# Interleaving transposes with low-part attention products, and splitting four more half heads, in a fused attention and MoE kernel on one Trainium2 core

## Chip, cores and metric

One core of a Trainium2 chip runs the whole kernel. The metric is the device time of one execution in microseconds (us); less is better.

## What is computed

The reference runs causal attention with a distance bias, then two feed-forward blocks, on 4 batches x 8 heads x 576 positions x 64 dimensions:

```python
scores = scale * np.matmul(q, k.transpose(0, 1, 3, 2))
cum = np.cumsum(np.maximum(s, 0.0), axis=-1)
bias = -(cum[:, :, :, None] - cum[:, :, None, :])
scores = np.where(causal, -1000000000.0, scores + np.minimum(bias, 0.0))
scores = scores - np.max(scores, axis=-1, keepdims=True)
attn = np.exp(scores)
attn = attn / (np.sum(attn, axis=-1, keepdims=True) + 1e-09)
x = np.matmul(attn, v)          # -> 2304 tokens x 512
h = ((x @ w1) * (x @ w2)) @ w3  # 1024 wide
x = h @ w_out                   # 512
h = x @ w_in                    # 2048
out = (h - np.tanh(h)) @ w_out2
```

## The kernel before

**Numbers.** Nearly all products run as fp32r matmuls on values split in two parts: a high part (a rounded copy) and a low part (value minus high part), made by a copy on ACT or DVE and a subtraction on DVE or POOL (`split`). The first batch's attention is the exception: there the heads run in full fp32 (`full`), which needs no split, and each fp32 product is shown as two matmuls in the trace.

**Attention.** A head has five tiles of queries (`QT`: 64, 128, 128, 128, 128 rows), in two groups: group 0 is tiles 0 to 2 (queries 0 to 319), group 1 is tiles 3 and 4. Per tile: the scores go to one of two PSUM banks (L589 when full, L591 and L592 when split); DVE adds the mask and takes the row minimum (L602); ACT takes the exponential (L608) into the buffer `e`; `flip` transposes `e` in chunks of 128 columns on TensorE (L638) into one of three banks, up to four to a bank, and copies them out to `en` (full) or splits them to `eh` and `el`. Per group, `pv` then multiplies by the values: full, L673 on `en`; split, first the high part on `eh` with 128 stationary columns (the two parts of V side by side, L675), then the low part on `el` with 64 stationary columns (L678), three matmuls for group 0 (320, 256 and 128 columns wide) and five for group 1 (four of 256, one of 128). L685 adds the two halves of the bank.

**Order of heads.** Batch 0 runs group 0 of its eight heads, then group 1 of its eight heads, all full. Then come the heads of batch 1 (again group 0 of all, then group 1 of all) and of batches 2 and 3 (both groups together), all split. Split heads use two sets of buffers in turn; the set of the odd heads lies in a pool that opens only when batch 0's heads are done. The products of a batch with w1 and w2 (`products`, L737, three matmuls of 288 columns to an operation) follow its attention at a lower priority, beside the next batch's attention. The weights w1 and w2 are decoded from doubles in 16 chunks (L431 to L437: one ACT and four DVE instructions each, then a split) at priorities around those of the first heads: the number `convp` sets where. After the attention come w3 folded into w_out, the product with that, and the second feed-forward block, which fills the span from about 590 us on.

**Who sets the order.** A planner (`Plan.order`) schedules the whole program with a cost for each operation, taking on each engine the ready operation of the lowest priority number; `emit` then writes the instructions in order of planned start. A `pv` or a bank of transposes is one operation. Where the planner finds TensorE idle in the first 150 us it puts in filler matmuls (L506), which compute nothing. Engines run in the order written.

Of the kernel before, what the change touches and what calls it, by code (L numbers as in the profile page):

```python
# [16 lines left out]
P = 128  # L17
B, H, S, D = 4, 8, 576, 64
# [16 lines left out]
XT = [(t, min(t + 512, NT)) for t in range(0, NT, 512)]  # L35
MASKED8 = -8.0e9
NR = D + 10
PARAM = dict(ramp0=50.0, ramp1=50.0, byf=(0,), dsub=1000.0, dsub0=1000.0, dcopy=1000.0, dcopy0=600.0, dother=1000.0, dother0=1000.0, spi=500.0, lay=6, lay0=4, layp=2.2e5, layf=2.95e5, gate=0, dve0=1000.0, early=100.0e3, raw0=0, rawp=-700.0, ng=3, nosb=2, cut=(1,), convq=1200.0, natb=8, abk=1, wap=0.95e6, dve=1000.0, act=0.0, pool=0.0, sem=160.0, pesem=180.0, slow=1.1, convp=590.0, npre=4,
             nbias=3, keep=0.5, ff=0.0, fu=150.0e3, wlast=8, bw=370.0, ntr=3, actb=1, actn=0, spp=-80.0, ne=2, nsb=2, ncf=5, outlag=15)

LO_CLAMP = 2.0 ** -15 * 1.125
# [19 lines left out]


class Op:
    __slots__ = ("opts", "eng", "lat", "fn", "prio", "deps", "succ", "n", "ready", "start", "end", "dur", "as_", "ae", "two", "kind", "bank")


class Plan:
# [11 lines left out]
        self.BIAS = {"DVE": PARAM["dve"], "ACT": PARAM["act"], "POOL": PARAM["pool"]}  # L79
        self.ops = []  # L80

    def op(self, opts, r=(), w=(), prio=0.0, lat=0.0, two=False, kind=None):
        o = Op()
        o.kind = kind
        o.two = two
        o.opts = {e: (d, fn) for e, d, fn in opts}
        o.prio, o.lat, o.eng = prio, lat, None
        o.bank = None
        for x, items in (("r", r), ("w", w)):
            if any((it[0] if isinstance(it, tuple) else it) is self.fill_bank for it in items):  # L90
                o.bank = x
        o.deps = set()
        for which, items in ((0, r), (1, w)):
            for it in items:
                b, parts = it if isinstance(it, tuple) else (it, range(it.n))
                for i in ([parts] if isinstance(parts, int) else parts):
# [12 lines left out]
        self.ops.append(o)  # L109
        return o  # L110
# [20 lines left out]
    def order(self):  # L131
# [34 lines left out]
        while True:  # L166
# [35 lines left out]
            if e == "PE":  # L202
                while self.fill_from < free[e] and free[e] + 110.0 < t < self.fill_until and not unread and free[e] >= read:
                    f = Op()
                    f.eng, f.fn, f.start, f.prio, f.lat, f.deps = e, self.filler, free[e], 9e9, 0.0, ()
                    f.dur = 107.0 * self.clock(free[e])
                    f.end = f.start + f.dur
                    self.busy(f.start, f.end)
                    done.append(f)
                    free[e] = f.end  # L210
                t = max(t, free[e])
# [22 lines left out]
        return sorted(range(len(done)), key=lambda i: (done[i].start, i))  # L234

    def emit(self):
        for i in self.order():
            self.done[i].fn()


def c_pe(n, m=P):
# [24 lines left out]
def tile_kernel(ctx, tc, qk, v, s, w1, w2, w3t, w_out, w_in, w_out2, out):  # L266
    nc = tc.nc
# [76 lines left out]
    def dve(fn, n, r, w, prio, fast=False, two=False, extra=0.0):  # L344
        pl.op([("DVE", c_dve(n, fast) + extra, fn)], r=r, w=w, prio=prio, two=two or fast)

    def pe(cost, fn, r, w, prio):
        pl.op([("PE", cost, fn)], r=r, w=w, prio=prio)


    nat = Pool("nat", "right")
# [187 lines left out]
    def head(h, full, groups=(0, 1)):  # L539
# [87 lines left out]
        def flip(t):  # L627
            q0, q1 = QT[t]
            nq = q1 - q0
            nch = (q1 + P - 1) // P  # L630
            p_ = pr + 10 * t + 50
            for js in [list(range(min(4, nch)))] + ([[4]] if nch > 4 else []):
                bk = tr_ring.next()
                rows = D if js == [4] else P

                def tr(bk=bk, js=js, rows=rows):
                    for n, c in enumerate(js):
                        nc.tensor.transpose(bk.t[:rows, n * P:(n + 1) * P], e.t[:, EOFF[t] + c * P:EOFF[t] + c * P + rows], ident.t)  # L638
                pe(109.0 * len(js), tr, [(e, t), ident], [bk], p_)
                n = len(js)  # L640
                if js == [4]:
                    view = lambda d: d.t[:D, eb + 1024:eb + 1024 + P]
                    src = lambda bk=bk: bk.t[:D, 0:P]
                else:
                    o = q0 if t < 3 else eb + q0 - 320
                    if n == 1:
                        view = lambda d: d.t[:, o:o + nq]
                        src = lambda bk=bk: bk.t[:, 0:nq]
                    else:
                        view = lambda d, n=n: d.t[:, o:o + 256 * n].rearrange("p (c q) -> p c q", q=256)[:, :, 0:nq]  # L650
                        src = lambda bk=bk, n=n: bk.t[:, 0:n * nq].rearrange("p (c q) -> p c q", q=nq)
                if full:
                    copy(lambda view=view: view(en), src, n * nq, [bk], [(en, t)], p_, psum=True)
                else:
                    split(lambda view=view: view(eh), (eh, t), lambda view=view: view(el), (el, t), src, n * nq, [bk], p_, psum=True)

        def pv(grp):
# [9 lines left out]
            X = xf[(h // 2) % 2]  # L667
            o = (h % 2) * D

            def mm():  # L670
# [5 lines left out]
                if not full:  # L676
                    for j, (c, a, w_, kk) in enumerate(lst):
                        nc.tensor.matmul(bk.t[:D, n - w_:n], V.t[:kk, c, 0:D], el.t[:kk, a:a + w_], start=False, stop=j == last, skip_group_check=True)  # L678
            if full:
                pe(sum(c_pe4(w_) for _, _, w_, _ in lst), mm, [RV, (en, parts)], [bk], p_)  # L680
                copy(lambda: X.t[o:o + D, q0:q0 + n], lambda: bk.t[:D, :n], n, [bk], [(X, h % 2)], p_, psum=True)
            else:
                pe(sum(c_pe(w_) + c_pe(w_, D) for _, _, w_, _ in lst), mm, [V, (eh, parts), (el, parts)], [bk], p_)
                copy(lambda: pvt.t[:, :n], lambda: bk.t[D:, :n], n, [bk], [pvt], p_, psum=True)
                dve(lambda: nc.vector.tensor_tensor(X.t[o:o + D, q0:q0 + n], bk.t[:D, :n], pvt.t[:, :n], op=ALU.add), n, [bk, pvt], [(X, h % 2)], p_)  # L685

# [62 lines left out]
                    [cs], [(c_d, b * 2 + half)], 0)  # L749

    for h in range(H):
        head(h, True, (0,))
    for half in range(2):
        for k in range(KC):
            for src, hb, lb in ((w1, w1h, w1l), (w2, w2h, w2l)):
# [5 lines left out]
    for h in range(H + 1):  # L761
        if h == PARAM["natb"]:
            nat.close()
            pl.op([("X", 0.0, lambda: None)], w=[eh])
            spl.open()
            constants(1)
        if h < H:
            head(h, h < PARAM["natb"], (1,))
    for b in range(B):
        if b + 1 < B:  # L770
            for g in ((0,), (1,)) if b + 1 in PARAM["cut"] else ((0, 1),):
# [182 lines left out]
```

## Time and profile before

| | |
|---|---|
| median of 3 runs | 980.98 us (977.44 to 984.19) |
| profiled execution | 975.06 us, span of its instructions 973.3 us |
| TensorE busy (matmul) | 958.5 us, 98% of the span, 5619 matmuls |
| DVE, ACT, POOL busy | 699.6 (72%), 597.6 (61%), 384.2 us (39%) |
| granted TensorE clock | 0.999 over the span |

"Busy" of TensorE counts a matmul from its first column to its last result; matmuls overlap, so what one costs is read from the distance between starts, not from its duration. The profiled execution is one run, 0.6% under the median of the three.

### The profile page before, as it was taken

Reading aid. Unit: us, or ns where it says so; the run is one execution under the profiler, and the core shown is the slowest. Engines: PE = TensorE matmul, PEld = TensorE weight load, DVE = VectorE, ACT = ScalarE, POOL = GpSimd, SP = SyncE. Lnnn points to the kernel's source line nnn. Section 1 sums busy time; section 2 is a strip of 40 time slices with the busy share of each in tenths; the row PEclk is TensorE's granted clock in tenths of the full one; section 3 lists DMA queues with packets and bytes.
Section 4 is the critical chain, followed back from the end, with each engine's and each line's share of the span. In section 5 each row is a group of like instructions: output and inputs, shape, how many; then the busy total and the mean of one; then the engine's idle time right before and its main releaser. Section 6 shows DMA issues by size and latency. Waiting matters only on the chain.

```text
span 973.3 us, 16442 instructions
## 1 busy us (share of the span) xinstructions
PE 958.5 (98%) x5619; PEld 832.9 (86%) x5619; DVE 699.6 (72%) x1421; ACT 597.6 (61%) x1360; POOL 384.2 (39%) x330
## 2 busy tenths in 40 slices
PE   8999999999999999999999999999999999999998
PEld 6667899999999999889888898878888888888897
DVE  7888868889889759996596897984454555454554
ACT  5777677888888744443444457555556555645565
POOL 3444566535535333422454548432222222222222
PEclk9999999999999999999999999999999999999999
DMA  6665455654545135568488782212003000200010
GB/s 184 187 189 173 132 169 180 200 193 124 174 143 158 45 105 178 176 204 285 136 312 286 249 274 81 65 55 77 1 0 110 21 1 1 87 0 1 1 44 23
DMA packets 69162, 122.22 MB, mean 126 GB/s; under 512 B 6651, under 2 KB 38656, under 8 KB 69078
## 3 DMA queue, kind: packets, MB, share of 16 engines
q1 hardware_dynamic: 69078, 121.17, 39.0%
q8 instruction: 44, 0.72, 0.3%
q14 instruction: 40, 0.33, 0.1%
HBM read 91.43 MB, written 25.99 MB: 121 GB/s over the span
## 4 chain that ended last, share of the span: by engine, by line
PE 89%; DVE 4%; DMA 3%; issue 2%; ACT 1%; POOL 1%; SPq 0%; DVEq 0%; ACTq 0%; POOLq 0%
PE bank L879 19%; PE bank L737 18%; PE bank L902 6%; PE bank L900 6%; PE bank L901 6%; PE bank L638 5%; PE bank L842 3%; PE bank L841 3%; PE bank L843 3%; PE bank L673 3%; PE bank L589 2%; PE bank L675 2%; PE bank L678 2%; PE bank L592 2%; PE bank L591 2%
## 5 line engine op out<-in xcount | busy, mean ns | idle before, releaser
L334 POOL TENSOR_TENSOR gl<-pg,gh 128x512 fp32r<-128x512 f32 (+1 forms) x78 | 98.8, 1266 | 260.8 <-ACT gh L328 234.3
L879 PE MATMUL bank<-x2b,wih 128*128 128x512 f32 (+1 forms) x640 | 182.4, 370 | 0.0
L890 DVE TENSOR_TENSOR pg<-bank,u 128x512 f32<-128x512 f32 (+1 forms) x80 | 50.8, 635 | 142.1 <-ACT th L889 138.0
L879 PEld LDWEIGHTS bank<-x2b,wih 128*128 128x128 f32 x640 | 116.7, 188 | 21.7
L879 PE MATMUL bank<-x2b,wil 128*128 128x512 f32 (+1 forms) x320 | 117.9, 368 | 0.0
L902 PE MATMUL bank<-voh,gl 128*128 128x512 f32 x288 | 113.1, 393 | 0.4 <-POOL gl L334 0.4
L900 PE MATMUL bank<-voh,gh 128*128 128x512 f32 x288 | 113.0, 392 | 0.2 <-ACT gh L328 0.2
L901 PE MATMUL bank<-vol,gh 128*128 128x512 f32 x288 | 112.6, 391 | 0.0
L328 ACT ACTIVATE gh<-pg 128x512 fp32r<-128x512 f32 (+1 forms) x80 | 47.1, 589 | 87.0 <-DVE pg L894 85.9
L608 ACT ACTIVATE e<-e,nmx 64x64 f32<-64x64 f32 (+4 forms) x160 | 88.6, 555 | 7.6 <-DVE nmx L602 6.9
L887 ACT ACTIVATE u<-bank 128x512 f32<-128x512 f32 (+1 forms) x80 | 44.4, 555 | 71.6 <-PE bank L879 65.4
L737 PE MATMUL bank<-xh,w2h 128*128 128x288 f32 x256 | 81.4, 318 | 1.3 <-DVE cst L745 1.3
L737 PE MATMUL bank<-xh,w1h 128*128 128x288 f32 x256 | 81.3, 318 | 0.7 <-ACT asb L328 0.5
L602 DVE CUSTOM_DVE_ANT_0 e<-bank,msk 64x64 f32<-64x64 f32 (+4 forms) x160 | 64.4, 418 | 21.1 <-PE bank L592 14.0
L431 ACT ACTIVATE wt<-wraw 128x512 f32<-128x512 f32 x72 | 47.9, 670 | 50.5 <-DMA wraw<-w_out 14.1
L638 PE MATMUL bank<-ident,e 128*128 128x128 f32 (+1 forms) x480 | 78.5, 274 | 0.2
L737 PE MATMUL bank<-xh,w2l 128*128 128x288 f32 x256 | 75.5, 295 | 0.0
L737 PE MATMUL bank<-xh,w1l 128*128 128x288 f32 x256 | 75.5, 295 | 0.0
L737 PE MATMUL bank<-xl,w1h 128*128 128x288 f32 x256 | 75.5, 295 | 0.0
L737 PE MATMUL bank<-xl,w2h 128*128 128x288 f32 x256 | 75.4, 295 | 0.0
L894 DVE COPY_PREDICATED pg<-mk,th 128x512 f32<-128x512 uint32 (+1 forms) x80 | 62.6, 783 | 13.6 <-ACT mk L892 5.7
L879 PEld LDWEIGHTS bank<-x2b,wil 128*128 128x128 f32 x320 | 60.3, 188 | 10.5
(139 smaller groups left out, 2589.2 us busy)
## 6 DMA issues: line engine op xcount, KB each, us to landing
rqk<-qk SPq DMA_DIRECT2D x24, 576.0 KB
wraw<-w_out SPq DMA_DIRECT2D x24, 512.0 KB
c_d<-cst SPq DMA_DIRECT2D x32, 288.0 KB
wraw<-w SPq DMA_DIRECT2D x16, 512.0 KB
wraw<-w3t SPq DMA_DIRECT2D x16, 512.0 KB
cf<-c_d SPq DMA_DIRECT2D x32, 256.0 KB
wraw<-w_in SPq DMA_DIRECT2D x16, 512.0 KB
x_d<-x2s SPq DMA_DIRECT2D x16, 512.0 KB
```

Of the source, the lines that this page charges most:

```text
L334: o.append(("POOL", c_pool2(n), lambda: nc.gpsimd.tensor_tensor(dst(), a(), b().bitcast(F32), op=ALU.subtract)))
L431: act(lambda: nc.scalar.activation(tf(), h32().bitcast(F32), AF.Abs), 512, [r_], [t_], prio)
L602: nc.vector.tensor_tensor_reduce(e.t[:nq, EOFF[t] + k0:EOFF[t] + k1], bk.t[:nq, :k1 - k0], bi.t[:nq, bo + k0:bo + k1], -0.125, 3.0e38 if f ...
L608: act(lambda: nc.scalar.activation(et(), et(), AF.Exp, bias=nmx.t[:nq, i, tm:tm + 1], scale=-1.0, accum_out=ssum.t[:nq, pj, t, i:i + 1]), ...
L638: nc.tensor.transpose(bk.t[:rows, n * P:(n + 1) * P], e.t[:, EOFF[t] + c * P:EOFF[t] + c * P + rows], ident.t)
L737: nc.tensor.matmul(bk.t[:, :HALF], w_.t[:, k, f * P:(f + 1) * P], x_.t[:, k, o:o + HALF], start=k == 0 and j == 0, stop=k == KC - 1 and j ...
L879: nc.tensor.matmul(bk.t[:, :w], w_.t[:, k, a], X2.t[:, i, k, :w], start=k == 0 and n == 0, stop=k == KC - 1 and n == 2)
L890: dve(lambda u=u, pg=pg, hp=hp, c_=c_: nc.vector.tensor_tensor(c_(pg), hp(), c_(u), op=ALU.mult), w, [bk, u], [pg], pr)
L894: dve(lambda pg=pg, mk=mk, th=th, c_=c_: nc.vector.copy_predicated(c_(pg), c_(mk).bitcast(U32), c_(th)), w, [mk, th], [pg], pr, two=True)
L900: nc.tensor.matmul(bank[n].t, gh.t[:, a], voh[f].t, start=f == 0, stop=False)
L901: nc.tensor.matmul(bank[n].t, gh.t[:, a], vol[f].t, start=False, stop=False)
L902: nc.tensor.matmul(bank[n].t, gl.t[:, a], voh[f].t, start=False, stop=f == NF2 - 1)
```

## The change

Three things change. First, `flip` and `pv` hand the planner their parts: each transpose by itself, and a split `pv` as its high part and a list of low matmuls. `emit` then looks, for each split `pv`, at the next 8 operations on TensorE in the planned order (`ahead=8`). A bank of transposes among them is moved up if by the plan its data (and its bank) are there by the end of that `pv` (`zipw=1.0`), until there are as many transposes as low matmuls. The high part is written first, and then low matmuls and transposes in turn; the planned times stay as they are. Second, four half heads of batch 0 are split instead of full: group 0 of head 6 (`part0=(6,)`) and group 1 of heads 2, 4 and 6 (`part1=(2, 4, 6)`). Third, `convp` goes from 590 to 690, which puts the decoding of w1 and w2 later by one head's priority.

```diff
     def emit(self):
-        for i in self.order():
-            self.done[i].fn()
+        seq = [self.done[i] for i in self.order()]
+        pe = [o for o in seq if o.eng == "PE" and o.fn is not self.filler]
+        at = {o: max([d.end + d.lat + (0.0 if d.eng == "PE" else self.SEM["PE"]) for d in o.deps], default=0.0) for o in pe if o.kind == "tr"}
+        idx = {o: n for n, o in enumerate(seq)}
+        used, zipped = set(), {}
+        for i, a in enumerate(pe):
+            if a.kind != "pv":
+                continue
+            turns = []
+            for b in pe[i + 1:i + 1 + PARAM["ahead"]]:
+                if len(turns) >= len(a.parts[1]) or any(d in pe[i + 1:i + 1 + PARAM["ahead"]] and d not in used for d in b.deps):
+                    break
+                if b.kind == "tr" and b not in used and a not in b.deps and at[b] <= a.start + PARAM["zipw"] * a.dur and all(idx[d] < idx[a] for d in b.deps):
+                    turns += b.parts
+                    used.add(b)
+            zipped[a] = turns
...
+        for o in seq:
+            if o in zipped:
+                first, last = o.parts
+                first()
+                for n in range(max(len(last), len(zipped[o]))):
+                    for x in (last, zipped[o]):
+                        if n < len(x):
+                            x[n]()
+            elif o not in used:
+                o.fn()
...
     for h in range(H):
-        head(h, True, (0,))
+        head(h, h not in PARAM["part0"], (0,))
...
-            head(h, h < PARAM["natb"], (1,))
+            head(h, h < PARAM["natb"] and h not in PARAM["part1"], (1,))
```

## Rows read from the trace of the kernel before

**Rows 1.** The page's list of engines: busy us, share, instructions.

```profile
PE 958.5 (98%) x5619; PEld 832.9 (86%) x5619; DVE 699.6 (72%) x1421; ACT 597.6 (61%) x1360; POOL 384.2 (39%) x330
```

**Rows 2.** Stretches: length, then busy us (instructions) of each engine; clock, DMA.

```profile
25.00:50.00 25.00, 23.62 (x158) 16.25 (x157) 20.27 (x58) 19.23 (x62) 10.70 (x11) 1.00 0.63 184
50.00:75.00 25.00, 24.44 (x147) 17.39 (x146) 22.01 (x49) 19.52 (x45) 10.78 (x12) 1.00 0.69 196
75.00:100.00 25.00, 25.00 (x148) 18.77 (x148) 21.80 (x55) 18.49 (x48) 12.44 (x12) 1.00 0.53 157
100.00:125.00 25.00, 24.45 (x191) 22.83 (x190) 20.12 (x56) 15.53 (x53) 14.17 (x17) 1.00 0.47 131
...
425.00:450.00 25.00, 24.44 (x164) 22.90 (x163) 18.69 (x32) 9.61 (x18) 8.54 (x6) 1.00 0.88 286
```

**Rows 3.** Stretches of 50 to 100 us, fillers (L506) alone, summed.

```profile
sum 50.00, PE 2.34 PEld 1.90; mean PE 0.47 PEld 0.38
```

**Rows 4.** Matmuls in order of time, 68 to 74 us: start, us, name.

```profile
68.69 2.16 PE L673 MATMUL bank<-en,rv 128*64 128x256 f32 x10
70.78 0.66 PE L638 MATMUL bank<-ident,e 128*128 128x128 f32 x4
71.27 0.92 PE L589 MATMUL bank<-rqk 69*128 69x448 f32 x2
72.03 0.27 PE L617 MATMUL bank<-ident,ssum 128*4 128x128 f32 x1
...
72.58 0.65 PE L589 MATMUL bank<-rqk 69*128 69x288 f32 x2
73.06 0.27 PE L638 MATMUL bank<-ident,e 128*64 128x128 f32 x1
```

**Rows 5.** Matmuls in order of time, 255 to 262 us: the same pieces, split.

```profile
255.45 0.30 PE L591 MATMUL bank<-kh,qs 128*128 128x288 f32 x1
...
255.72 0.30 PE L737 MATMUL bank<-xh,w2h 128*128 128x288 f32 x1
...
256.79 0.69 PE L675 MATMUL bank<-eh,vs 128*128 128x256 f32 x5
257.31 0.69 PE L678 MATMUL bank<-el,vs 128*64 128x256 f32 x5
257.85 0.49 PE L638 MATMUL bank<-ident,e 128*128 128x128 f32 x3
...
261.00 0.37 PE L591 MATMUL bank<-kh,qs 128*128 128x448 f32 x1
...
261.41 0.27 PE L638 MATMUL bank<-ident,e 128*64 128x128 f32 x1
```

**Rows 6.** DVE groups of 150 to 340 us: count, busy us, mean ns, idle before.

```profile
L332 DVE TENSOR_TENSOR el<-bank,eh 128x512 fp32r<-128x512 f32 x45 | 29.5, 680 | 0.5 <-ACT eh L328 0.3
...
L685 DVE TENSOR_TENSOR xf<-bank,pvt 64x256 f32<-64x256 f32 x23 | 9.5, 412 | 6.5 <-ACT pvt L328 6.2
...
L332 DVE TENSOR_TENSOR el<-bank,eh 64x128 fp32r<-64x128 f32 x23 | 6.4, 277 | 0.1
```

**Rows 7.** Waits of TensorE in 0 to 160 us: total, times, longest.

```profile
PE bank L589 <- DMA rqk<-qk: 1.0, 2, 0.6
```

**Rows 8.** Weight loads in order of time, 258 us, behind three transposes.

```profile
258.06 0.14 PEld L591 LDWEIGHTS bank<-kh,qs 128*64 128x64 f32 x1
258.17 0.14 PEld L592 LDWEIGHTS bank<-kl,q 74*64 74x64 f32 x1
258.23 0.19 PEld L591 LDWEIGHTS bank<-kh,qs 128*128 128x128 f32 x1
258.34 0.19 PEld L592 LDWEIGHTS bank<-kl,q 74*128 74x128 f32 x1
```

**Rows 9.** Matmuls at 254 us: three low matmuls, then one transpose.

```profile
254.00 0.48 PE L678 MATMUL bank<-el,vs 128*64 128x320 f32 x3
254.32 0.28 PE L638 MATMUL bank<-ident,e 128*128 128x128 f32 x1
```

**Rows 10.** Weight load that starts when the product behind that transpose does.

```profile
254.44 0.19 PEld L737 LDWEIGHTS bank<-xl,w2h 128*128 128x128 f32 x1
```

**Rows 11.** All transposes of attention: what TensorE sat idle for before them.

```profile
  ACT e L608: 0.3, 2
```

More of the change, by code (lines that the diff above doesn't have):

```diff
@@ L37 @@
 NR = D + 10
-PARAM = dict(ramp0=50.0, ramp1=50.0, byf=(0,), dsub=1000.0, dsub0=1000.0, dcopy=1000.0, dcopy0=600.0, dother=1000.0, dother0=1000.0, spi=500.0, lay=6, lay0=4, layp=2.2e5, layf=2.95e5, gate=0, dve0=1000.0, early=100.0e3, raw0=0, rawp=-700.0, ng=3, nosb=2, cut=(1,), convq=1200.0, natb=8, abk=1, wap=0.95e6, dve=1000.0, act=0.0, pool=0.0, sem=160.0, pesem=180.0, slow=1.1, convp=590.0, npre=4,
+PARAM = dict(ahead=8, zipw=1.0, part0=(6,), part1=(2, 4, 6), ramp0=50.0, ramp1=50.0, byf=(0,), dsub=1000.0, dsub0=1000.0, dcopy=1000.0, dcopy0=600.0, dother=1000.0, dother0=1000.0, spi=500.0, lay=6, lay0=4, layp=2.2e5, layf=2.95e5, gate=0, dve0=1000.0, early=100.0e3, raw0=0, rawp=-700.0, ng=3, nosb=2, cut=(1,), convq=1200.0, natb=8, abk=1, wap=0.95e6, dve=1000.0, act=0.0, pool=0.0, sem=160.0, pesem=180.0, slow=1.1, convp=690.0, npre=4,
              nbias=3, keep=0.5, ff=0.0, fu=150.0e3, wlast=8, bw=370.0, ntr=3, actb=1, actn=0, spp=-80.0, ne=2, nsb=2, ncf=5, outlag=15)
@@ L63 @@
 class Op:
-    __slots__ = ("opts", "eng", "lat", "fn", "prio", "deps", "succ", "n", "ready", "start", "end", "dur", "as_", "ae", "two", "kind", "bank")
+    __slots__ = ("opts", "eng", "lat", "fn", "prio", "deps", "succ", "n", "ready", "start", "end", "dur", "as_", "ae", "two", "kind", "bank", "parts")
 class Plan:
@@ L80, in __init__, with op @@
         self.ops = []
-    def op(self, opts, r=(), w=(), prio=0.0, lat=0.0, two=False, kind=None):
+    def op(self, opts, r=(), w=(), prio=0.0, lat=0.0, two=False, kind=None, parts=None):
         o = Op()
+        o.parts = parts
         o.kind = kind
@@ L204, in order @@
                     f = Op()
+                    f.kind = f.parts = None
                     f.eng, f.fn, f.start, f.prio, f.lat, f.deps = e, self.filler, free[e], 9e9, 0.0, ()
@@ L236, in emit @@
     def emit(self):
-        for i in self.order():
-            self.done[i].fn()
+        seq = [self.done[i] for i in self.order()]
[14 more added lines that the diff above has]
+            zipped[a] = turns
+        self.nzip = (len(used), sum(min(len(a.parts[1]), len(t)) for a, t in zipped.items()), len(zipped))
+        for o in seq:
[8 more added lines that the diff above has]
+                o.fn()
 def c_pe(n, m=P):
@@ L345, in dve, with pe @@
         pl.op([("DVE", c_dve(n, fast) + extra, fn)], r=r, w=w, prio=prio, two=two or fast)
-    def pe(cost, fn, r, w, prio):
-        pl.op([("PE", cost, fn)], r=r, w=w, prio=prio)
+    def pe(cost, fn, r, w, prio, kind=None, parts=None):
+        pl.op([("PE", cost, fn)], r=r, w=w, prio=prio, kind=kind, parts=parts)
     nat = Pool("nat", "right")
@@ L634, in flip, with tr @@
                 rows = D if js == [4] else P
[L636 to L639, printed above, removed]
+                def tr(bk=bk, rows=rows, n=0, c=0):
+                    nc.tensor.transpose(bk.t[:rows, n * P:(n + 1) * P], e.t[:, EOFF[t] + c * P:EOFF[t] + c * P + rows], ident.t)
+                trs = [lambda tr=tr, n=n, c=c: tr(n=n, c=c) for n, c in enumerate(js)]
+                pe(109.0 * len(js), lambda trs=trs: [f() for f in trs], [(e, t), ident], [bk], p_, kind="tr", parts=trs)
                 n = len(js)
@@ L668, in pv, with low @@
             o = (h % 2) * D
+            def low(j, c, a, w_, kk):
+                nc.tensor.matmul(bk.t[:D, n - w_:n], V.t[:kk, c, 0:D], el.t[:kk, a:a + w_], start=False, stop=j == last, skip_group_check=True)
+            lows = [lambda j=j, x=x: low(j, *x) for j, x in enumerate(lst)]
             def mm():
@@ L675, in mm @@
                         nc.tensor.matmul(bk.t[:, n - w_:n], V.t[:kk, c, :], eh.t[:kk, a:a + w_], start=j == 0, stop=False, skip_group_check=True)
-                if not full:
-                    for j, (c, a, w_, kk) in enumerate(lst):
-                        nc.tensor.matmul(bk.t[:D, n - w_:n], V.t[:kk, c, 0:D], el.t[:kk, a:a + w_], start=False, stop=j == last, skip_group_check=True)
             if full:
@@ L682, in pv @@
             else:
-                pe(sum(c_pe(w_) + c_pe(w_, D) for _, _, w_, _ in lst), mm, [V, (eh, parts), (el, parts)], [bk], p_)
+                pe(sum(c_pe(w_) + c_pe(w_, D) for _, _, w_, _ in lst), lambda: [f() for f in [mm] + lows], [V, (eh, parts), (el, parts)], [bk], p_, kind="pv", parts=(mm, lows))
                 copy(lambda: pvt.t[:, :n], lambda: bk.t[D:, :n], n, [bk], [pvt], p_, psum=True)
```

## The prediction

> **What bounds the kernel now.** I read the list of engines first: the matmul engine is busy for 98% of the span, the next one, DVE, for 72% [rows 1]. Then I cut the span into stretches, because a share over 973 us hides stages. TensorE is full in all of them but the first 50 us [rows 2]; what it can lose is work or filler, not waiting. The attention of the later batches never lets it idle, since the products with w1 and w2 stand behind every head at a lower priority and fill the gaps. So a microsecond of matmul work removed anywhere after some 50 us shortens the kernel by about that, as long as there is other work ready in its place. The end of the stage in which the products finish, 425 to 450 us, bears this out: DVE is at 18.69 of 25 us there and TensorE at 24.44 [rows 2], so the stage ends on matmuls. Between 50 and 100 us, where three of the four half heads stand, TensorE is full too, with 2.34 us of fillers in it [rows 3]; but DVE is at 22.01 and 21.80 of 25 us [rows 2], its heaviest stretch of that part of the kernel.
>
> **The half heads of group 1 (heads 2, 4 and 6).** Full, one costs TensorE from start to start: the ten value matmuls 70.78 - 68.69 = 2.09 us, the scores of 448 columns 72.03 - 71.27 = 0.76, and twice the scores of 288 columns, 73.06 - 72.58 = 0.48 each [rows 4]. That is 2.09 + 0.76 + 0.96 = 3.81 us. Split, the same pieces cost 257.31 - 256.79 = 0.52 (high) and 257.85 - 257.31 = 0.54 (low), 261.41 - 261.00 = 0.41 for 448 columns and twice 255.72 - 255.45 = 0.27 [rows 5]: 2.01 us. The transposes are the same. The saving is 1.80 us each, 5.4 us in all, on the engine that is full.
>
> Against it stands DVE. A split half head adds two subtractions out of PSUM of 0.68 us and one of 0.28 (only DVE does these), and the addition of the two halves, 0.41 [rows 6]: 2.05 us, 6.2 us for three. Copies of q, k and v, and their subtractions, go to ACT and POOL for the most part, which have 12 and 27 us idle in 50 to 100 us [rows 2]. DVE has 3.0 + 3.2 = 6.2 us idle there [rows 2]. It would fill them exactly if the stretch stayed as long as it is, and the stretch is to become 5.4 us shorter. So some DVE work must move behind 100 us, where 4.9 of the next 25 us are idle [rows 2]; the decoding of weights can move, since it feeds products and not the heads, and `convp` moves it. What can't move is the order within a head: the row minimum waits behind a subtraction on DVE, the exponential behind that, the transposes behind both. Ends: nothing of the 5.4 us is lost, or all of it (TensorE then runs fillers or waits, for DVE). Products ready to fill are few here, because those of the second half of the rows need all heads of this group. I take 2.0 us as lost, near the shorter end, because the decoding can be put off.
>
> The DMA queue of SP: a split half head of group 1 loads 576 KB of q and k instead of 288, and it has one load each of `kl` and `q2` where the full one has two of `rel`, so the count is the same. The load of `q2` waits for a copy, and behind it in SP's order stand the next heads' loads and the weights. DMA is at 0.69 and 0.53 of its time [rows 2], and 0.9 MB more at 180 GB/s are 5 us of 50; I price it at nothing, with up to 1 us if a head waits as two did at the start [rows 7].
>
> **Head 6 of group 0.** It has 576 columns of scores where a group 1 has 448 + 288 + 288 = 1024, and 704 of values where that has 1152, so by estimate it saves TensorE 0.6 of the 1.80 us, 1.1 us. It stands at 37 to 50 us, where matmuls wait for the heads' own chain (25 to 50 us is TensorE's emptiest full stretch, 23.62 with fillers counted as busy [rows 2]). A shorter matmul there becomes a filler, and DVE gets some 0.6 x 2.05 = 1.2 us more. I price it at nothing, between -1.1 and +1.2 us. Moving the decoding later by one head costs nothing while products are not short, up to 1.5 us if the few products that run before 60 us come later.
>
> **The turns.** The question is what a transpose costs, and where. The three transposes at 257.85 us are 0.11 us apart: the third starts with its successor's load at 258.06 [rows 5, 8]. Is that its stream or its load? A load runs while the matmul ahead of it streams, and the next load starts when its own matmul takes over the array. Behind the third transpose stands a matmul with 64 stationary columns, whose load starts at 258.06; it takes over at 258.17, when the next load starts [rows 8]. It is 64 wide and holds the array for 0.06 us, its successor's load being 64 wide; the one after it holds 0.11, with a load of 128 columns behind it [rows 8]. So a load of 64 columns needs at most 0.06 us, and yet the transpose ahead of such a load held 0.11: that is its own stream. From the other side, a single transpose between three low matmuls and a product starts at 254.32 and the product takes over at 254.44 [rows 9, 10]; the low matmuls keep their 0.32 us, although the last streams only 128 columns and would not have hidden a load of 0.11.
>
> The low matmul of 256 columns costs (0.54 - 0.06) / 4 = 0.12 us, its stream, its load of 64 columns hidden. In turns, then: low 0.12 with the transpose's load behind it, transpose 0.11 with a low load behind it. In groups it is the same 0.12 + 0.11. **The turns save nothing on TensorE.** What is left is an end effect: the last low matmul (0.06 us) hides a transpose's load but not one of 128 columns (0.11), so 0.05 us hangs on what follows each of 48 low groups. Most are followed by a transpose before; after, those with fewer transposes than low matmuls are not. At most 0.05 x 48 = 2.4 us either way, and since gains and losses mix I take 0.
>
> The turns add a risk. A transpose is written as soon as the first low matmul, when its data need only be there by the planned end of the `pv`, some 0.4 us later. If it is late, TensorE stands, and everything behind it, since it runs in order. Before, transposes waited for the exponential twice, 0.3 us in all [rows 11], so data are mostly early. Ends: 0 and 52 x 0.4 = 21 us; I take 0.5 us, next to the row.
>
> **Sum.** -5.4 + 2.0 + 0 + 0 + 0.5 = -2.9 us on the profiled execution's 975.06 us, 972.2 us. The median of the runs lies 5.9 us above that execution, so I predict 980.98 - 2.9 = 978.1 us. The runs spread over 6.7 us; 1% (9.8 us) is about what a measurement of this kernel can tell from no change.
>
> **Rivals.** (a) *The load is what a transpose waits for.* Then in turns its load hides under a low matmul's stream and a transpose costs about 0.055 us, saving 0.055 per pair. There are at most 4 pairs in a group 1 and 2 in a group 0: 24 x 6 + 14 = 158, 8.7 us; with partners for two in three, 5.8 us, giving 980.98 - 2.9 - 5.8 = 972.3 us. For it speaks that 0.11 us is also exactly what a load of 128 columns takes [rows 8]; against it, the transpose that held 0.11 ahead of a 64-column load. The Trainium skill, TensorE: Matmul & The Clock Gate, section LDWEIGHTS, says that a load lasts as long as its columns at 1.2 GHz, whatever the rows; by that a transpose's 128 columns would be the 107 ns between transposes, and this rival would hold. The trace agrees for the scores and not for the transposes. Chance 0.15.
>
> (b) *DVE takes the place of TensorE between 50 and 110 us.* The saved matmul time turns into fillers and waits for the row minimum or for `el`; DVE's 6.2 us of new work against 6.2 us of idle time decide. The time would be 981 us, or up to 2 us more with head 6's part. Chance 0.25.
>
> (c) *Transposes stand in front of their data.* The place is TensorE's order in each `pv`; the price is up to 0.4 us for each of 52. From 0.06 us each it eats the gain of 2.9 us, at 0.3 us each the kernel needs 980.98 - 3.4 + 15.6 = 993 us, slower than before. For it speaks that the planner's times are estimates and that the window admits data that come at the end of the `pv`; against it, the two short waits before. Chance 0.08.
>
> (d) *Few turns happen* (most transposes near a `pv` belong to tiles not ready): then (a) and (c) shrink and the sum stays, which is why it has no price of its own.
>
> **How the numbers follow.** My forecast has a chance of 0.5, rival (b) 0.25, (a) 0.15, (c) 0.08, the rest something else. The forecast's own range, with the terms' ends and the spread of runs, is 973 to 983. With (a) below and (b) above, and the near part of (c), 967 to 986 holds eight in ten. Faster by over 1% (under 971.2) needs (a) with nearly all pairs, or all terms at their good ends: 0.17. Slower by over 1% (over 990.8) needs (c): 0.08. Within 1%: 0.75.
>
> **What the profile after would show.** Right: 36 matmuls of L673 fewer (ten for each group 1, six for head 6), no idle time before L638 to speak of, low matmul and transpose together still 0.22 to 0.23 us in turns, products starting earlier than before from 60 us on, DVE above 22 of 25 us between 50 and 100 us with the decoding ending some microseconds later. A pair of 0.17 us in turns would prove (a). More than 5 us of fillers and waits in 50 to 110 us would prove (b); idle time before L638 named after the exponential would prove (c). The prediction goes wrong most easily in the size of what DVE gives back.

## The result, and the profile after

The changed kernel takes 984.72 us (median of 7 runs, 981.74 to 991.98) against 978.14 us of the kernel before beside it (7 runs, 973.66 to 984.19): ratio 1.0067, 95% interval 1.0043 to 1.009. It is 6.6 us slower, where 2.9 us less was forecast. The profiled execution takes 984.89 us, span 983.2.

The list of engines [rows 1], and the stretches of 25 us [rows 2], of after:

```profile
PE 961.5 (98%) x5645; PEld 837.9 (85%) x5645; DVE 709.1 (72%) x1437; ACT 601.5 (61%) x1370; POOL 397.2 (40%) x344
```
```profile
25.00:50.00 25.00, 21.41 (x151) 14.93 (x149) 21.31 (x61) 17.55 (x56) 10.77 (x13) 1.00 0.65 190
50.00:75.00 25.00, 23.52 (x153) 17.50 (x152) 22.65 (x54) 19.49 (x48) 13.97 (x15) 1.00 0.65 193
75.00:100.00 25.00, 24.31 (x160) 20.34 (x159) 22.57 (x53) 19.73 (x49) 13.83 (x13) 1.00 0.66 193
100.00:125.00 25.00, 22.66 (x174) 20.41 (x173) 21.44 (x56) 17.48 (x54) 14.56 (x16) 0.93 0.46 133
```

TensorE is less busy in each of the four, by 0.7 to 2.2 us, and from 100 to 125 us its granted clock is 0.93. The idle time is new. What TensorE waited for from 25 to 160 us, of before and then of after (total, times, longest):

```profile
PE bank L592 <- DMA r_d<-rinv: 1.1, 1, 1.1
PE bank L589 <- DMA rqk<-qk: 1.0, 2, 0.6
...
PE bank L589 <- DVE nmx L602: 0.4, 1, 0.4
```
```profile
PE bank L619 <- DVE nmx L630: 1.4, 2, 1.0
PE bank L665 <- ACT e L636: 1.2, 3, 0.5
PE bank L620 <- DMA q<-qs: 1.2, 2, 0.7
PE bank L617 <- DVE nmx L630: 1.2, 3, 0.6
...
PE bank L699 <- DVE el L360: 0.7, 1, 0.7
```

Before, the row minimum (`nmx`) kept TensorE waiting for 0.4 us; after it is 2.6, with 1.2 for the exponential, 0.7 for `el` and 1.2 for the copy of q: all steps of a head's own chain. TensorE runs in the order written, so such a wait shows where the plan had put no other work in front. The matmuls of the products in each stretch, of before and of after:

```profile
75.00:100.00 25.00, 7.77 (x39) 5.80 (x39) 1.00 0.53 157
100.00:125.00 25.00, 17.05 (x105) 14.43 (x105) 1.00 0.47 131
```
```profile
75.00:100.00 25.00, 10.82 (x60) 8.73 (x60) 1.00 0.66 193
100.00:125.00 25.00, 10.99 (x62) 9.48 (x61) 0.93 0.46 133
```

After, 60 instead of 39 products run while the heads of group 1 still go on, and 43 fewer in the 25 us behind. They are taken early and then gone: the second half of the rows needs the last heads. All engines in the same 10 us, first of before, then of after:

```profile
110.00:115.00 5.00, 5.00 (x40) 4.79 (x41) 4.67 (x13) 3.77 (x14) 2.70 (x5) 1.00 0.24 65
115.00:120.00 5.00, 4.53 (x39) 4.35 (x37) 2.57 (x10) 2.75 (x10) 1.54 (x2) 1.00 0.60 158
```
```profile
110.00:115.00 5.00, 3.02 (x21) 2.30 (x20) 4.96 (x15) 2.52 (x8) 4.25 (x5) 1.00 0.71 200
115.00:120.00 5.00, 4.64 (x25) 4.36 (x24) 3.27 (x9) 3.46 (x13) 1.78 (x3) 0.66 0.25 68
```

TensorE runs 21 matmuls instead of 40, and the clock then falls: 0.66 over the next 5 us, which mixes the levels of 2.4 and 1.2 GHz. I call this place the hole. In it, in order of time:

```profile
108.19 1.91 PE L534 MATMUL bank<-msk 128*128 128x128 bf16 x31
...
112.53 0.84 DVE L461 TENSOR_SCALAR wt<-wt 128x512 uint32<-128x512 uint32 x1
113.29 0.21 DVE L630 CUSTOM_DVE_ANT_0 e<-bank,msk 64x64 f32<-64x64 f32 x1
...
113.56 0.42 PE L619 MATMUL bank<-kh,qs 128*128 128x320 f32 x1 [0.96 <-DVE nmx L630]
```

First 31 fillers, and later a wait of 0.96 us for a row minimum that stood behind a decoding step on DVE. With 0.72 us for `el` and 0.30 for a DMA into `q`, which stand between them, that is all of the 2.0 us in which TensorE is idle from 110 to 115 us.

The heads' chain itself is read from the last exponential of group 0 and of group 1 in batch 0 (ACT, in order of time), of before and of after:

```profile
44.58 0.56 ACT L608 ACTIVATE e<-e,nmx 128x320 f32<-128x320 f32 x1
...
95.75 0.77 ACT L608 ACTIVATE e<-e,nmx 128x576 f32<-128x576 f32 x1
```
```profile
50.92 0.55 ACT L636 ACTIVATE e<-e,nmx 128x320 f32<-128x320 f32 x1
...
100.47 0.77 ACT L636 ACTIVATE e<-e,nmx 128x576 f32<-128x576 f32 x1
```

Group 1 takes 51.17 us before and 49.55 after: with 5.4 us less matmul work it is 1.6 us shorter, and it starts 6.3 us later (about 3.1 of these are there at 30 us, when the engines have run the same instructions in the same order; last section).

### The profile page after: what moved, and what is told of

It reads as the page before. It is cut to its first block, busy times and chain, and to the rows that moved or that the text cites. A ratio compares the mean times of both kernels' runs of the same rounds, so it can differ in the third digit from the quotient of the medians.

```text
span 983.2 us, 16561 instructions
## 1 busy us (share of the span) xinstructions
PE 961.5 (98%) x5645; PEld 837.9 (85%) x5645; DVE 709.1 (72%) x1437; ACT 601.5 (61%) x1370; POOL 397.2 (40%) x344
## 4 chain that ended last, share of the span: by engine, by line
PE 86%; DVE 5%; DMA 4%; ACT 2%; issue 2%; POOL 1%; SPq 0%; ACTq 0%; DVEq 0%; POOLq 0%
PE bank L908 19%; PE bank L766 17%; PE bank L931 6%; PE bank L929 6%; PE bank L930 6%; PE bank L665 5%; PE bank L872 3%; PE bank L871 3%; PE bank L870 3%; PE bank L707 2%; PE bank L699 2%; PE bank L620 2%; PE bank L619 2%; PE bank L832 1%; PE bank L834 1%
## 5 line engine op out<-in xcount | busy, mean ns | idle before, releaser
L665 PE MATMUL bank<-ident,e 128*128 128x128 f32 (+1 forms) x480 | 87.5, 277 | 2.1 <-ACT e L636 1.2
L360 DVE TENSOR_TENSOR el<-bank,eh 128x512 fp32r<-128x512 f32 (+1 forms) x156 | 70.3, 471 | 4.0 <-ACT eh L356 3.1
L923 DVE COPY_PREDICATED pg<-mk,th 128x512 f32<-128x512 uint32 (+1 forms) x80 | 62.7, 784 | 13.6 <-ACT mk L921 5.7
```

The costliest lines, as they stand in the source:

```text
L360: o = [("DVE", c_dve(n), lambda: nc.vector.tensor_tensor(dst(), a(), b().bitcast(F32), op=ALU.subtract))]
L923: dve(lambda pg=pg, mk=mk, th=th, c_=c_: nc.vector.copy_predicated(c_(pg), c_(mk).bitcast(U32), c_(th)), w, [mk, th], [pg], pr, two=True)
```

## The experiments

**The theory after the result.** Until about 115 us the heads' chain (scores, row minimum, exponential, transposes, copies) bounds the kernel, and products only fill TensorE's gaps in it. Less head work means that products are taken earlier; their stock runs out before the last head's values are there, and the saved time returns as fillers, waits and half clock. **Rivals:** DVE is the bound; the turns cost it; the old order was merely lucky.

**The parts alone.** Each is the changed kernel with other parameters; medians with the kernel before beside it.

```diff
 # changed:   ahead=8, part0=(6,), part1=(2, 4, 6), convp=690
+# zip only:  ahead=8, part0=(),   part1=(),        convp=590
+# split only:ahead=0, part0=(6,), part1=(2, 4, 6), convp=690
+# part1 only:ahead=0, part0=(),   part1=(2, 4, 6), convp=590
+# part0 only:ahead=0, part0=(6,), part1=(),        convp=590
+# decode:    ahead=0, part0=(),   part1=(),        convp=690
+# one half:  ahead=0, part0=(),   part1=(2,),      convp=690
+# early:     ahead=0, part0=(6,), part1=(2, 4, 6), convp=690, convq=800
```

> Turns alone: no half head of the first batch is split and the decoding stands where it stood. Theory A (the new head 6 of group 0 is what costs, the turns cost little): ratio to before 1.000 to 1.003, at most 2 us slower, idle time before the transposes about 1 us against 0.2. Theory B (transposes in front of their data set the loss): 5 to 7 us slower, ratio 1.005 to 1.007. Rival (a) of the prediction (a transpose waits for its load): 5 to 9 us faster.

> The four split half heads and the later decoding, with the transposes in their old places. Theory A: 3 to 6 us slower than before (ratio 1.003 to 1.006), with the loss between 35 and 50 us and between 105 and 150 us. Theory B: 3 us faster, as the prediction had it (ratio 0.997).

> Group 1 of heads 2, 4 and 6 split alone, decoding where it stood, no turns. If the matmul time saved (5.4 us) comes through less what DVE gives back: 2 to 5 us faster (ratio 0.995 to 0.998). If DVE or the chain of a head takes all of it, as rival (b) has it: no change, or 2 us slower.

> Group 0 of head 6 split alone, decoding where it stood, no turns. Theory A: 2 to 4 us slower (ratio 1.002 to 1.004), the exponential of that head's first tile 3 to 4 us later than before. Otherwise: no change within 1 us.

> Only the decoding of w1 and w2 moved by one head's priority, all heads of batch 0 full, no turns. If the later decoding costs by itself: 2 to 4 us slower. If it is neutral and only matters beside split heads: within 1.5 us of the kernel before.

> Only group 1 of head 2 split, decoding later, no turns. If every split half head costs about the same: 1 to 2 us slower than before. If one fits into DVE's idle time: 1 to 2 us faster.

> As e2, with the second half of the weights decoded four heads earlier in priority (convq 800 for 1200), so that more products can be ready when batch 0 ends. Theory C: the hole at 100 to 125 us is filled with products of the second half of the columns, 2 to 4 us faster than e2. Theory D: DVE has still more to do between 50 and 100 us, 2 to 4 us slower than e2.

| run | median | before | ratio (95%) |
|---|---|---|---|
| turns alone | 982.6 | 979.72 | 1.0027 (1.0007 to 1.0047) |
| four half heads and `convp` | 983.28 | 979.72 | 1.0048 (1.0028 to 1.0068) |
| group 1's three, `convp` 590 | 989.69 | 979.72 | 1.0097 (1.0071 to 1.0123) |
| head 6 of group 0, `convp` 590 | 986.17 | 979.72 | 1.0069 (1.0043 to 1.0095) |
| `convp` 690 alone | 978.08 | 980.0 | 0.9989 (0.9969 to 1.0009) |
| one half head split, `convp` 690 | 977.37 | 979.86 | 0.9986 (0.9966 to 1.0006) |
| four half heads, second matrix half decoded earlier | 988.06 | 979.83 | 1.0086 (1.0057 to 1.0116) |

The two halves of the change add up: 2.7 + 4.8 = 7.5 thousandths against 6.7. Every kernel that splits head 6's group 0, or group 1 of more than one head, is slower. The later decoding alone changes nothing; beside the split it seems to make the loss smaller (4.8 thousandths with it, 9.7 and 6.9 for the two parts without it), but no run has all four half heads at `convp` 590. Three results are worse than any case that was put down: group 1's three lose 10 us where at most 2 were thought of, head 6 alone 6.5 where at most 4 were, and the earlier decoding 4.8 us more than the four half heads at the medians, where 2 to 4 was the case of a DVE that sets the pace. (In the run with one half head split, the full heads 4 and 6 read bias rows that its load has overwritten; the work is the same.)

**Less TensorE work, early and late.** The kernel before, with four of five value chunks left out of group 1's `pv` (so the output lacks them): in heads 2, 4 and 6 of batch 0, and, in a second run, in six heads of batch 2. Each run has one of the two conditions; the microseconds are estimates.

```diff
+            if full and grp == 1 and h in (2, 4, 6):    # early: 4.9 us
+            if grp == 1 and 16 <= h < 22:               # late: 5.2 us
+                lst = lst[:1]
```

> The kernel before, with four of the five chunks of the value product left out in group 1 of heads 2, 4 and 6 (their output lacks those keys): eight matmuls less each, some 1.6 us of TensorE each and 4.9 us in all, nothing else changed. The premise of the prediction (TensorE sets the pace between 50 and 100 us, so matmul time saved there is time saved): 4 to 5 us faster, ratio 0.995. If the heads' own chain sets the pace there and the products fill the rest: under 2 us faster, with more fillers and waits in 50 to 110 us.

> The kernel before with four of five value chunks left out of group 1's low parts and high parts of heads 0 to 5 of batch 2, in the middle of the attention, where the first batch's cut left out as much. TensorE has 4 x 0.1 + 4 x 0.12 = 0.88 us less for each, 5.2 us in all. Theory (a saved microsecond of matmul work counts only where products stand ready to take its place, which they do here and not at the end of batch 0): 3 to 5.5 us faster, ratio 0.9945 to 0.997, granted clock 0.99 or more after 25 us. Rival (any cut upsets the planned order, or TensorE is not the bound in this stretch either): no gain or a loss, ratio 0.999 to 1.007.

Early: 987.1 us against 980.0, ratio 1.007 (1.0045 to 1.0096). Late: 975.46 against 980.16, ratio 0.9945 (0.9918 to 0.9971). The same cut, alone, costs 7 us at one place and gives all of its 5 us at the other. This is the pair that decides: the early cut has neither split nor added DVE work. The loss itself was not expected: the range was from 5 us faster to no gain. The profiled execution of the early cut took 992.83 us, the longest of its eight (983.48 to 992.83), so what it shows is deeper than at the median. Its products (matmuls in each stretch), and then its engines:

```profile
75.00:100.00 25.00, 10.74 (x63) 8.58 (x63) 1.00 0.61 166
100.00:125.00 25.00, 8.24 (x34) 6.55 (x33) 0.73 0.34 96
```
```profile
100.00:125.00 25.00, 18.85 (x98) 16.12 (x97) 17.24 (x43) 14.87 (x46) 11.31 (x13) 0.73 0.34 96
```

63 products in the first stretch and 34 in the second, where before had 39 and 105; TensorE 6 us idle, clock 0.73. The late cut keeps before's pattern, with 36 and 102:

```profile
75.00:100.00 25.00, 6.83 (x36) 5.34 (x36) 1.00 0.60 174
100.00:125.00 25.00, 16.93 (x102) 13.94 (x102) 1.00 0.47 133
```

**Holding the products back.** Four half heads split, and 72 product matmuls of batch 0's first half of the rows (f = 1 to 3) held until the exponential of head 7's tile 3, the first of its two in group 1 (shortened):

```diff
+                    hold = [late] if b == 0 and half == 0 and f in (1, 2, 3) else []
-                    pe(..., [(XH, xs), (XL, xs), (wh, parts), (wl, parts)], [bk], pos)
+                    pe(..., hold + [(XH, xs), (XL, xs), (wh, parts), (wl, parts)], [bk], pos)
```

> As e2, but 72 of the 96 products of the first half of batch 0's rows are held back in the plan until head 7's exponential of group 1, so that they stand ready when the last head of batch 0 is finishing. If the saved matmul time is spent on these products early and comes back as a hole at 100 to 120 us (with the granted clock falling to half in it): 3 to 6 us faster than e2, no fall of the clock there. If DVE is the cause alone: no faster than e2, or slower, since fillers only move from one place to the other.

986.44 against 979.86, ratio 1.0081 (1.006 to 1.0101). The hole at 110 us is filled and the time isn't better: 82 fillers run behind 50 us, against 38 in before, so the idle time only stands earlier. The theory had forecast 3 to 6 us less than the four half heads alone; it is 3.2 us more at the medians. So holding these products back doesn't bring the time back. That work is missing, and not order, is the likely reading; it isn't shown.

**The stock of products.** By the kernel's order, 114 product matmuls of batch 0 (96 for the first half of the rows, 18 for the second) can run before the values of heads 6 and 7 in group 1 are there (their copy into `xh`), and the 115th can't. The copy, the 114th and the 115th in order of time, of before and then of after:

```profile
108.39 0.42 ACT L328 ACTIVATE xh<-xf 128x256 fp32r<-128x256 f32 x1
...
108.63 0.30 PE L737 MATMUL bank<-xh,w2l 128*128 128x288 f32 x1
...
110.81 0.38 PE L737 MATMUL bank<-xh,w1h 128*128 128x288 f32 x1
```
```profile
108.05 0.29 PE L766 MATMUL bank<-xh,w2l 128*128 128x288 f32 x1
...
113.12 0.42 ACT L356 ACTIVATE xh<-xf 128x256 fp32r<-128x256 f32 x1 [0.65 <-POOL xf L740]
...
114.37 0.38 PE L766 MATMUL bank<-xh,w1h 128*128 128x288 f32 x1
```

Between the two products lie 2.2 us before and 6.3 after. In the traces of the late cut, of `convp` 640 and 690 and of both runs that move transposes and split nothing it is 2.2 too, and 0.1 with less decoding on full heads; none of these is slower than 2.7 thousandths. In the eleven kernels that lose 4.8 thousandths or more with no product held, it is 4.4 to 11.4 us (11.4 in the early cut). So the stock does run out early in the kernels that lose. The sizes don't go together, and two kernels don't fit: one half head split has 5.7 us and loses nothing, the held products have 0.6 and lose 8.1 thousandths.

**DVE.** Added: in heads 2, 4 and 6 the full kernel gets a split one's subtractions and additions, some 6.2 us by estimate, first out of the PSUM banks, then out of SBUF, so that no bank is held. Taken away: the four DVE decoding steps of the second half of w1 and w2 left out, beside full and beside split half heads (DVE's busy time falls by 23.2 us with full heads, from 697.1 to 673.9, and by 13.6 with split ones, from 710.3 to 696.7). And the split kernel without the low parts in batch 0 (fewer matmuls, no `el`). The lines are shortened:

```diff
+  sub(lo(el), bank, en); tensor_tensor(pvt, bank, X)      # from PSUM
+  sub(lo(el), en, en);   tensor_tensor(pvt, X, X)         # from SBUF
+  if light[0]: return t_       # before the decoding's four DVE steps
+  lows = [...] if b else []    # batch 0 has the high part alone
```

> The kernel before, with the DVE work of a split half head added to group 1 of heads 2, 4 and 6 and no TensorE work saved: three subtractions out of PSUM and one addition each, 2.05 us, 6.2 us in all. If DVE's load is what eats the saving (rival b): 4 to 7 us slower than before. If it is not DVE but the way a split head is prepared: 0 to 2 us slower.

> The kernel before with the same extra DVE subtractions and additions in heads 2, 4 and 6 of batch 0 as the run that added DVE work, but reading from SBUF, so that no PSUM bank is held until they are done. Some 6 us of DVE work more, nothing more for TensorE. If the loss of 11.6 us there came from banks held longer (the length of a head's own chain): within 2.5 us of before, ratio 0.9975 to 1.0025. If it came from DVE's load: 6 to 12 us slower, ratio 1.006 to 1.012.

> All heads of batch 0 full, decoding later (as e8), no turns, and the four DVE steps of decoding left out for the second half of w1 and w2 (8 chunks, some 25 us of DVE between 50 and 115 us; those weights are not the reference's). Beside e14 it asks whether DVE's share decides if saved TensorE time counts. If heads and TensorE pace 50 to 115 us together, it is 2 to 6 us faster than before, with products still short of filling the end of batch 0.

> The four split half heads (as e2), no turns, with the same DVE steps left out. Theory C (saved TensorE time is spent on the few products that are ready, and the end of batch 0 waits for the heads' own chain, whoever is busy): 2 to 6 us slower than e13, as e2 is to e8. Theory D (DVE's load decides): 3 to 6 us faster than e13, since now the 5.4 us of matmul time come through.

> As e2 (split half heads, later decoding, no turns), but the four split half heads of batch 0 leave out the low part of their probabilities: no subtraction out of PSUM on DVE and no low products (DVE 1.64 us less per half head of group 1, TensorE 0.54 us less). If DVE's load sets the loss: 4 to 7 us faster than e2, at or below the kernel before (977 to 980 us). If the hole at the end of batch 0 sets it, whatever DVE does: within 2 us of e2 (981 to 984).

| run | median | before | ratio (95%) |
|---|---|---|---|
| more DVE work, from PSUM | 991.89 | 980.0 | 1.0116 (1.0093 to 1.014) |
| more DVE work, from SBUF | 990.84 | 980.16 | 1.0117 (1.008 to 1.0154) |
| less decoding, full, `convp` 690 | 981.8 | 979.83 | 1.0022 (1.0002 to 1.0042) |
| less decoding, split | 987.18 | 979.83 | 1.0077 (1.005 to 1.0105) |
| split, no low part in batch 0 | 989.43 | 979.86 | 1.0121 (1.0091 to 1.015) |

The held banks are not the cause of the first loss: without them it is as large, and by its expectation that speaks for DVE's load. Without the low parts the kernel is 6 us slower than the four half heads, which neither of its two cases had; DVE's busy time over the span is 710.3 us in both, so it doesn't test DVE's load, and it is one more kernel with less TensorE work in these heads that loses. Engines with less decoding (split):

```profile
75.00:100.00 25.00, 25.00 (x173) 21.47 (x172) 18.57 (x51) 19.70 (x47) 11.70 (x12) 1.00 0.59 171
100.00:125.00 25.00, 20.19 (x140) 17.83 (x137) 14.62 (x52) 15.96 (x53) 13.00 (x17) 0.86 0.43 123
```

DVE has 6.4 and 10.4 us free there, and the split still costs 987.18 - 981.8 = 5.4 us. So DVE's busy share is not the bound. Yet DVE work added here costs: inside the heads more than its own time, and as earlier decoding 4.8 us. The time from the last exponential of group 0 to that of group 1:

| kernel | us |
|---|---|
| before; late cut | 51.2; 50.9 |
| after; four half heads | 49.6; 50.0 |
| early cut of TensorE | 52.9 |
| less decoding, full; split | 51.7; 52.0 |
| more DVE work, from PSUM; SBUF | 55.2; 55.9 |

TensorE work taken out and decoding taken out move it by less than 2 us; DVE steps inside the heads stretch it by 4 to 5 us. That fits a chain of dependent steps better than a full engine. Two things speak against so neat a reading. With head 6's group 0 split alone it is 56.0 us. And when the chain ends doesn't by itself set the time: with `convp` 690 alone the last exponential comes at 100.56 us, 4.8 later than before (1.6 of them are there at 30 us), and nothing is lost; with the four half heads it comes at 100.30, and 4.8 thousandths are lost.

**Copying, and another old order.** The split kernel with `q2`'s high part made by a copy instead of a DMA behind a copy; and the kernel before with `convp` 640.

```diff
+            if b == 0:
+                copy(lambda: Q2.t[:D, qa:qb], lambda: rq()[:D, qa:qb], qb - qa, [R], [(Q2, 0)], p_)
-convp=590
+convp=640
```

> Split half heads and later decoding without turns (as e2), but the high part of q that goes to the second score operand is made by a copy on ACT or DVE for batch 0, and not by a DMA from the first copy. If the waits for that DMA (copy, issue on SP, 2 us to land, before the head's first score) make the loss: 3 to 5 us faster than e2, at or under the time of the kernel before. If they only show where other waits would stand: within 1 us of e2 (983 us).

> The kernel before with the decoding's priority half way (640 for 590), no other change: a new plan of the same work. It shows how much a mere new order moves the time: if the order before was good by chance, 2 to 5 us slower; if plans of the same work differ little, within 1.5 us.

986.61 against 980.0, ratio 1.0069 (1.0043 to 1.0096): the DMA of `q2` is not the cost. 977.75 against 979.86, ratio 0.9986 (0.9969 to 1.0002): with the order changed and the work kept, nothing is lost, nor with `convp` 690; as far as these two orders show, the old one was not just lucky.

**The turns.** The moved transposes written behind all low matmuls, not in turn with them; nothing split.

```diff
-                for n in range(max(len(last), len(zipped[o]))):
-                    ...
+                for f in last + zipped[o]:
+                    f()
```

> As e1 (turns alone), but the transposes that are moved up stand behind all low matmuls and not between them. If the turns gain something by standing between (a load hidden): 2 us or more slower than e1. If it is only the end effect and early waits that cost: 0.5 to 2 us faster than e1, within 1.5 us of before; a low part is then followed by a transpose more often, at 0.06 us for 0.11.

979.15 against 979.83, ratio 1.0000 (0.9978 to 1.0021). Moving transposes up shows no cost; the turn itself would cost what the turns alone cost, 2.7 thousandths or some 2.65 us, for 80 pairs 0.03 us each. The intervals of the two runs overlap (1.0007 to 1.0047 there), so this difference is likely but not clear of noise.

## Why the prediction was wrong

**The step that failed is the first part's rule**, that a microsecond of matmul work removed anywhere after some 50 us shortens the kernel by about that. It rested on the later batches and the end of the products' stage, where it holds: the late cut gave 4.7 us at the medians, 0.0055 x 980.16 = 5.4 by the ratio, for 5.2 us of work. It was carried over to 50 to 110 us because TensorE was full there [rows 2]. Full with what was not asked: with products that had no need to run yet. The prediction even said that products are few here, and used it for the size of a give-back and not for the rule. (Nor is TensorE full in all other stretches, as it said: before has it at 23.43 of 25 us from 125 to 150, and 23.40 from 300 to 325.) The early cut shows the rule false there with nothing else changed.

**Group 1's 5.4 us** left as work. L673 had 128 matmuls and L705 has 92, the 36 fewer that were foretold. With each matmul priced at the median distance between starts of its kind ahead of the same successor, over both traces, the work with all four half heads is 6.1 us less (920.1 in the split kernel, 926.2 in the one with `convp` 690 alone). What is left of the two spans, fillers, waits and half clock, is 9.8 us more (57.2 against 47.4), +3.7 in all; the spans differ by 982.5 - 978.7 = 3.8 us and the medians by 5.2. **The give-back, taken as 2.0 us, measured 9.8**, for all four half heads. By stretch, 1.7 us of it lie in 25 to 50 us, 1.3 in 50 to 75, 4.0 in 100 to 125 and 2.0 in 125 to 150.

**Rival (b)** had the direction, and 981 to 983 us. It named DVE as the bound; the runs with less decoding speak against DVE's busy share, though added DVE work does cost. Its own mark, over 5 us of fillers and waits in 50 to 110 us, is met by the fillers' 4.52 us and 2.1 us of waits. But before has 3.18 of fillers there too, and 31 of after's 60 fillers in it stand at 108 us, at the hole; some 6 of the 9.8 us lie behind 100 us, at a place that no case had.

**Head 6 of group 0**, priced at nothing within 1.2 us, costs 6.9 thousandths alone, at `convp` 590. Its first exponential comes at 46.9 us against 38.3, 5.5 us later than the lag that the run already had; part of that is made up by 50 us.

**The SP queue and the later decoding** were priced at nothing, rightly for the decoding (0.9989); the DMA of `q2` did keep TensorE waiting for 1.2 us, but without it the time is no better.

**The turns on TensorE**: the working was right, the price too low (0.5 us; the turns alone measured 2.65, between 0.7 and 4.6 by the interval). A pair still costs 0.22 to 0.23 us. After, in the first split half head of group 1, in order of time:

```profile
75.49 0.69 PE L707 MATMUL bank<-eh,vs 128*128 128x256 f32 x5
76.02 0.28 PE L699 MATMUL bank<-el,vs 128*64 128x256 f32 x1
76.14 0.27 PE L665 MATMUL bank<-ident,e 128*128 128x128 f32 x1
76.16 0.36 PE L699 MATMUL bank<-el,vs 128*64 128x256 f32 x1
76.36 0.27 PE L665 MATMUL bank<-ident,e 128*128 128x128 f32 x1
76.39 0.36 PE L699 MATMUL bank<-el,vs 128*64 128x256 f32 x1
76.59 0.27 PE L665 MATMUL bank<-ident,e 128*128 128x128 f32 x1
```

Transposes start 0.22 and 0.23 us apart, so nothing is saved by the turns, and rival (a) is false. The Trainium skill, TensorE: Matmul & The Clock Gate, section LDWEIGHTS, on whose rule for the length of a load rival (a) leaned, says that a load lasts by its columns; the spacing of these transposes does not come from their load, since a pair in turns costs no less than the 0.12 + 0.11 us in groups. The end effect, taken as 0 within 2.4 us, went the bad way: with the turns alone, the last low matmul is followed by a score or a product whose load has 128 columns 27 times, where it was 13 before. From the start of that load to the next one's it then holds the array for 0.108 us, instead of 0.060 ahead of a transpose. That is 14 x 0.048 = 0.7 us of the 2.65; the rest was not traced to rows.

**Early data.** Idle time of TensorE and its loads before transposes, put down to the exponential [rows 11], with the turns alone, with the half heads alone and after, one line each:

```profile
  ACT e L636: 0.7, 4
```
```profile
  ACT e L636: 6.1, 9
```
```profile
  ACT e L636: 3.8, 10
```

Rival (c) put such waits down to the turns. They come with the half heads; the turns alone add 0.4 us, near the 0.5 taken.

The base hides part of the miss: the kernel before measured 980.98 us then and 978.14 beside the changed one, so the time missed by 6.6 us where the change missed by 9.5. That the range of 967 to 986 us held the time is luck in part: rival (b) and the near part of (c) were in it, but on the base of 980.98 the ratio of 1.0067 gives 987.6.

**What stays open.** That less matmul work gains nothing there is shown; why it loses 5 to 7 us and not zero is shown by place and not by cause. A hole with the clock at half, a chain that starts later and later waits of products for their banks all stand in the traces, and no run parts them. The clock is not all of it: 0.93 over 25 us in after is at most 0.07 x 25 = 1.8 us by estimate, and of the early cut's eight runs the four with a mean clock of 0.996 or 0.997 still take 983.5 to 987.4 us.

## What to carry to other kernels

A full engine bounds a stretch only if what fills it can't run elsewhere: take the filler out of the count, and ask what the engine would do once the stock of ready work is used up. Removed work is worth its time where other work stands ready until the stage ends; where other work is waiting for the end of a chain of dependent steps, it was worth nothing here, and DVE steps added to that chain cost more than their own time (some 11 us for 6.2). An order written in turns is worth a test by itself, with the same moves made in groups beside it.

## What the runs showed of the hardware

The clock's first rise differs from run to run of the same instructions. The stretches from 5 to 25 us of the early cut, which equals the kernel before up to there:

```profile
5.00:10.00 5.00, 3.74 (x34) 3.22 (x34) 4.62 (x23) 0.66 (x1) 0.29 (x1) 0.80 0.93 292
10.00:15.00 5.00, 4.77 (x19) 2.38 (x17) 2.70 (x9) 4.04 (x10) 3.35 (x2) 0.50 0.70 227
15.00:20.00 5.00, 5.00 (x24) 3.57 (x24) 3.05 (x8) 1.86 (x8) 0.63 (x1) 0.50 0.09 26
20.00:25.00 5.00, 5.00 (x34) 3.44 (x33) 2.05 (x7) 2.99 (x10) 1.27 (x1) 0.83 0.50 158
```

Half clock lasts there until beyond 20 us; with head 6's group 0 split alone the stretch of 10 to 15 us has 0.89 already. The 14th exponential comes at 30.37 us in before and 3.07 us later in after; TensorE, DVE, ACT and POOL run the same instructions up to 34 us of before. That lag would account for most of the difference between the profiled spans (9.9 us) and the medians (6.6). After's own rows show 1.00 at the start, but its fillers start 0.107 us apart from 13 to 20 us, where before's start 0.056 apart, and it has 26 and 29 matmuls from 10 to 20 us, where before has 33 and 38: that is the lower level against the higher.

The other observation is what stood ahead of the lower clock later on: in the hole TensorE was idle for 2 us of 5, in three waits of 0.30 to 0.96 us, and the next 5 us have 0.66. The Trainium skill, TensorE: Matmul & The Clock Gate, section HAM oscillation — how this bites in real kernels, says that waits between groups of matmuls can throttle the clock, so that the next work starts slow. The hole agrees, with 25 matmuls in 115 to 120 us where before has 39, though the page's case is of longer waits, each for a DMA.
